# Batch 0 of a fused attention and expert kernel: transposed scores, normalisation by small products, a later read-out, one more DMA transpose, and a first weight chunk loaded in quarters

## The chip, the cores and the metric

The kernel runs on one core of one Trainium2 chip. The metric is the time on the device in microseconds (us); lower is better. Two kernels are compared by runs on the same chip in alternating rounds.

## The reference, cut to what matters

```python
# x (8 batches, 8 heads, 512 rows, 64), state (8, 8, 32, 64)
scores = scale * x @ state^T;  a = softmax(scores);   xread = a @ state        # 512 rows per batch
scores2 = scale * state @ x^T; a2 = softmax(scores2); sread = a2 @ x           # 32 rows per batch
y = concat([xread, sread], rows), heads side by side                           # (8 * 544, 512)
out = gelu(y @ w_in) @ w_out                                                   # w_in 512x2048, w_out 2048x512
```

Two facts shape the kernel. `scores2` is `scores` transposed, so one exponential E serves both reads. And `xread @ w_in` equals `a @ (state @ w_in)`, so the kernel multiplies the small `state` into `w_in` first (the tile P) and never forms `xread`.

## The kernel before

For each batch it computes E = exp(scores), normalises it to A, transposes A to AT, forms P, then `hp = P^T AT` (L470), its GELU `g`, and `op = g^T w_out` (L519, or L564 for parts of batch 0). `sread` ("the read-out") takes E and x to sums of 32 rows. All loads of weights and x go out from GpSimd in one queue, in program order, and are written as bf16:

```python
    load_w_in(0, 512)            # first w_in chunk: two halves (t = 0, 1) of 64 partitions, 512 columns
    load_w_out(0)
    load_w_in(512, 1024)
    load_st(1, 2)
    def load_rest():
        load_x(1)
        load_w_out(1)
        for f in range(2, FC):
            load_w_in(512 * f, 512 * f + 512)
            load_w_out(f)
        ...
```

Batch 0 is prepared in four parts of two heads. Rows of x lie on partitions, so the sum for the normalisation runs along the free dimension, on VectorE; GpSimd multiplies one half, and A is then transposed on TensorE:

```python
    def scores0(q):
        pc = ps_o.tile([128, SJ, 2 * NS], FP32, name="pc", tag="op")
        for j in range(SJ):
            nc.tensor.matmul(pc[:, j, :], lhsT=xT0[:, q, j, :], rhs=sb0[...], start=True, stop=True)
        nc.scalar.activation(out=part0(A.e, q), in_=pc, func=AF.Exp, scale=scale)
    def norm0(t):
        nc.vector.reciprocal(out=ics, in_=A.sums)          # sums from nc.vector.reduce_sum
        eng = nc.gpsimd if t == 0 else nc.vector
        eng.tensor_tensor(out=<A of half t>, in0=<E of half t>, in1=ics.to_broadcast(...), op=ALU.mult)
    def xtr_dma(b):                                        # later batches transpose x and A by DMA
        nc.sync.dma_start_transpose(out=A.xT..., in_=A.x4...)
```

The order of work around the read-out of batch 0 and the burst of P chunks:

```python
    xtr(1, (0, 1)); xtr(1, (2, 3))      # x of batch 1, needs its load
    sread(0); sread_out(0)              # read-out of batch 0
    M(7); scores(1, 0); scores(1, 1)
    srt(0)
    U(4, 5)                             # op, needs the second w_out piece
    rearr_ones(1)
    U(6)
    pmat(0, 2)                          # P from the third w_in piece
    ...
    burst([(1, 3), (2, 0), (2, 1)])     # at 40 us
```

The softmax here doesn't subtract the row's maximum and nothing guards it: scores larger than these inputs give would overflow.

## Time and profile before

| | kernel before |
|---|---|
| time, median of 3 runs | 215.29 us (215.14 to 215.52) |
| profiled span | 213.6 us |
| TensorE busy | 209.2 us, 98% of the span |
| first w_in halves landed | 8.28 and 9.63 us |
| second w_out piece landed | 21.14 us |
| third w_in piece, two halves landed | 22.00 and 23.28 us |

The page of a profile gives busy times and the chain that ended last; the chain of waits lists that chain's pieces in time as start, duration, engine, tile, line and count. A line such as L519 is the kernel's own. The prediction below shows the first 24 us of this chain. For the later reading these pieces are needed as well; they are from the chain of the kernel before:

```profile
23.93 0.34 PE p_ps L408 x8
24.27 0.97 PE op L519 x4
...
39.99 0.77 PE p_ps L408 x24
40.76 0.97 PE op L519 x4
```

The third w_in piece is used at 23.93 and had landed at 23.28, so TensorE had 0.65 us to spare there. The burst at 39.99 runs its 24 products without a gap.

### The profile page before, as it was taken

Reading aid. Unit: us, or ns where it says so; the run is one execution under the profiler, and the core shown is the slowest. Engines: PE = TensorE matmul, PEld = TensorE weight load, DVE = VectorE, ACT = ScalarE, POOL = GpSimd, SP = SyncE. Lnnn points to the kernel's source line nnn. Section 1 sums busy time; section 2 is a strip of 40 time slices with the busy share of each in tenths; the row PEclk is TensorE's granted clock in tenths of the full one; section 3 lists DMA queues with packets and bytes.
Section 4 is the critical chain, followed back from the end, with each engine's and each line's share of the span. In section 5 each row is a group of like instructions: output and inputs, shape, how many; then the busy total and the mean of one; then the engine's idle time right before and its main releaser. Section 6 shows DMA issues by size and latency. Waiting matters only on the chain.

```text
span 213.6 us, 4028 instructions
## 1 busy us (share of the span) xinstructions
PE 209.2 (98%) x1674; PEld 103.7 (49%) x1674; DVE 81.3 (38%) x169; ACT 122.5 (57%) x218; POOL 43.5 (20%) x57
## 2 busy tenths in 40 slices
PE   8999999999999999999999999999999999999994
PEld 7735444444444445444444444444444444765443
DVE  3835675723059102940177006900393026000151
ACT  3765855797777448844974467645864444864000
POOL 7573304901213013302321230300000000000000
PEclk9999999999999999999999999999999999999999
DMA  7999999983722691439350963170222014000034
GB/s 182 172 200 205 206 193 161 220 178 51 96 98 101 122 123 50 150 60 144 47 196 4 155 90 139 60 146 5 98 100 54 0 40 158 3 0 0 10 105 183
DMA packets 39731, 22.98 MB, mean 108 GB/s; under 512 B 22048, under 2 KB 36384, under 8 KB 39712
## 3 DMA queue, kind: packets, MB, share of 16 engines
q0 software_dynamic: 13664, 8.23, 27.8%
q1 hardware_dynamic: 25360, 14.09, 24.6%
q10 hardware_dynamic: 688, 0.39, 0.6%
q8 instruction: 13, 0.21, 0.4%
q14 instruction: 6, 0.05, 0.1%
HBM read 17.30 MB, written 8.91 MB: 123 GB/s over the span
## 4 chain that ended last, share of the span: by engine, by line
PE 97%; POOL 0%; ACT 0%; issue 0%; DVE 0%
PE op L519 47%; PE hp L470 25%; PE p_ps L408 4%; PE op L564 3%; PE hps L534 3%; PE ops L546 3%; PE warm_ps L133 2%; PE opl L497 2%; PE pt L316 2%; PE sr L371 1%; PE hp L624 1%; PE aT_ps L353 1%; PE xT_ps L239 1%; POOL a L303 0%; PE xT_ps L258 0%; PE pc L279 0%
## 5 line engine op out<-in xcount | busy, mean ns | idle before, releaser
L519 PE MATMUL op<-w_out_bf,g 128*128 128x512 bf16 x464 | 110.1, 379 | 0.0
L477 ACT ACTIVATE g<-hp 128x512 bf16<-128x512 f32 x124 | 66.5, 600 | 52.8 <-PE hp L470 52.7
L519 PEld LDWEIGHTS <-g 128*128 128x128 bf16 x464 | 44.9, 98 | 54.3 <-issue 1.5
L470 PE MATMUL hp<-AT,P 128*128 128x512 bf16 x248 | 63.4, 379 | 0.0
L483 DVE COPY osb<-op 128x512 f32<-128x512 f32 x31 | 21.4, 691 | 85.0 <-PE op L519 85.0
L470 PEld LDWEIGHTS <-P 128*128 128x128 bf16 x248 | 22.8, 98 | 25.2 <-ACT P L419 0.5
L419 ACT CAST P<-p_ps 128x512 bf16<-128x512 f32 x31 | 16.3, 595 | 12.5 <-PE p_ps L408 12.5
L420 DVE CAST P<-p_ps 128x512 bf16<-128x512 f32 x31 | 19.9, 682 | 6.0 <-PE p_ps L408 5.9
L202 POOL COPY x<-xb 128x1024 bf16<-128x1024 bf16 x12 | 12.2, 1043 | 31.9 <-DMA xb<-in_x_dram 26.5
L212 POOL COPY xo<-xb 128x1024 bf16<-128x1024 bf16 x12 | 12.2, 1049 | 21.7 <-PE sr L371 21.7
L336 DVE TENSOR_REDUCE cs<-e 128x16 f32<-128x512 bf16 x14 | 9.5, 678 | 4.0 <-ACT e L323 4.0
L323 ACT ACT_TABLE_LOAD x7 | 9.0, 1283 | 1.8 <-issue 1.3
L408 PE MATMUL p_ps<-w_in_bf,sbd 64*32 64x512 bf16 x248 | 9.9, 381 | 0.0
L483 DVE COPY osb<-ops 128x512 f32<-128x512 f32 x2 | 1.4, 692 | 22.5 <-PE ops L546 22.5
L339 DVE TENSOR_TENSOR a<-e,ics 128x512 bf16<-128x512 bf16 x14 | 9.7, 692 | 0.5
L477 ACT ACT_TABLE_LOAD x7 | 9.0, 1283 | 0.1
L508 ACT COPY osb<-opl 128x128 f32<-128x128 f32 x1 | 0.3, 266 | 15.2 <-PE opl L497 15.2
L133 PE MATMUL warm_ps<-warm 128*128 128x128 bf16 x66 | 7.0, 275 | 1.0 <-DVE warm L80 1.0
L564 PE MATMUL op<-w_out_bf,g 128*128 128x512 bf16 x32 | 7.8, 380 | 0.0
L323 ACT ACTIVATE e<-pt 128x512 bf16<-128x512 f32 x14 | 7.6, 594 | 0.1
L534 PE MATMUL hps<-XSR,w_in_bf 128*128 128x256 bf16 x64 | 7.6, 273 | 0.0
L546 PE MATMUL ops<-w_out_bf,g_sr 128*128 128x512 bf16 x32 | 7.1, 379 | 0.0
(80 smaller groups left out, 118.9 us busy)
## 6 DMA issues: line engine op xcount, KB each, us to landing
out_dram<-osb SPq DMA_DIRECT2D x24, 256.0 KB, 2.3
xb<-in_x_dram POOLq DMA_DIRECT2D x7, 512.0 KB, 6.2
w_in_bf<-in_moe_w_in_dram POOLq DMA_DIRECT2D x8, 256.0 KB, 10.1
w_out_bf<-in_moe_w_out_dram POOLq DMA_DIRECT2D x4, 512.0 KB, 11.6
out_dram<-osb SPq DMA_DIRECT2D x14, 128.0 KB, 2.0
x0f<-in_x_dram SPq DMA_DIRECT2D x2, 256.0 KB, 3.5
out_dram<-osb SPq DMA_DIRECT2D x8, 64.0 KB, 1.7
x0f<-in_x_dram ACTq DMA_DIRECT2D x1, 256.0 KB, 4.2
```

The lines of the kernel that those rows point to most:

```text
L202: nc.gpsimd.tensor_copy(out=A.x4[:, :, :, 64 * t:64 * t + 64].rearrange("p j c d -> p c j d"), in_=src[:, t],)
L323: nc.scalar.activation(out=A.e[:, :, 64 * half:64 * half + 64], in_=pt.rearrange("p j t c n -> p (j t) (c n)"), func=AF.Exp, scale=scale,)
L408: nc.tensor.matmul(ps[t][32 * c:32 * c + 32, :], lhsT=sbd[64 * t:64 * t + 64, b, c, 32 * t:32 * t + 32], rhs=w_in_bf[64 * t:64 * t + 64, c ...
L419: nc.scalar.copy(out=dst[:, 0, :], in_=ps[0])
L420: nc.vector.tensor_copy(out=dst[:, 1, :], in_=ps[1])
L470: nc.tensor.matmul(hp, lhsT=Ps[b][:, t, m * 128:(m + 1) * 128], rhs=atts[b].AT[:, :, t, :], start=(t == 0), stop=(t == 1),)
L477: nc.scalar.activation(out=gs[b][:, m, :], in_=hp, func=AF.Gelu)
L483: nc.vector.tensor_copy(out=osb, in_=ps)
L519: nc.tensor.matmul(ps, lhsT=gs[b][:, m, j * 128:(j + 1) * 128], rhs=w_out_bf[:, m, :], start=(m == 0), stop=(m == MC - 1),)
L534: nc.tensor.matmul(hp, lhsT=w_in_bf[:, c, m * 128:(m + 1) * 128], rhs=XSR[:, c, :], start=(c == 0), stop=(c == HC - 1),)
L546: nc.tensor.matmul(ps, lhsT=g_sr[:, m, s * 128:(s + 1) * 128], rhs=w_out_bf[:, m, :], start=(m == 0), stop=(m == MC - 1),)
L564: nc.tensor.matmul(ops[b, j], lhsT=gs[b][:, m, j * 128:(j + 1) * 128], rhs=w_out_bf[:, m, :], start=(m == 0), stop=(m == MC - 1),)
```

## The change

Its intent is to shorten the preparation of batch 0 and to keep GpSimd out of it. The scores are computed transposed (state rows on partitions, x rows along the free dimension), so that E comes out as ET and AT needs no transposes. The sums over state rows are then products with a block of ones; the reciprocals, split into two bf16 parts, are spread over partitions by 32 small products per half. The read-out needs E the other way round; a DMA transpose supplies it, and the read-out moves to the burst at 40 us. The first w_in chunk is loaded in quarters.

```diff
-    load_w_in(0, 512)
+    load_w_in(0, 256, (0,))
+    load_w_in(256, 512, (0,))
+    load_w_in(0, 256, (1,))
+    load_w_in(256, 512, (1,))
 ...
     def scores0(q):
+        t = q // 2                     # pcs[t]: one [128, 512] tile per half
+        nc.tensor.matmul(pcs[t][h, :], lhsT=sb0[:, t, q % 2, ...], rhs=xT0[:, q, ...], ...)
+        if q % 2 == 1:
+            nc.scalar.activation(out=eT0[:, t, :], in_=pcs[t], func=AF.Exp, scale=scale)
+    def sums0(t):                      # 4 products with bones, then reciprocal and its remainder
     def norm0(t):
-        eng = nc.gpsimd if t == 0 else nc.vector
+        ps = ps_o.tile([128, S], FP32, name="rb", tag="op")
+        for j in range(SJ):
+            for i, r in enumerate((r0_hi(t), r0lo[:, t, :, :])):
+                for c in range(HC):
+                    nc.tensor.matmul(ps[32 * c:32 * c + 32, 128 * j:128 * j + 128],
+                        lhsT=r[:, j, c:c + 1].to_broadcast((128, NS)), rhs=ident, ...)
+        nc.vector.tensor_tensor(out=A.AT[:, :, t, :], in0=eT0[:, t, :]..., in1=ps..., op=ALU.mult)
+    def e0_dma():
+        nc.sync.dma_start_transpose(out=e0, in_=eT0.rearrange("p t s -> p (t s)"))
 ...
-    sread(0)
-    sread_out(0)
     M(7)
 ...
-    srt(0)
     U(4, 5)
 ...
     mm2_m(0, 11)
+    e0_dma()
     begin(2)
 ...
-    burst([(1, 3), (2, 0), (2, 1)])
+    burst([(1, 3), (2, 0), (2, 1)], 0)
```

Cut: tiles, the casts and evictions that change between ScalarE and VectorE, the counts of the filler products (`keep_warm`), the later place of `srt(0)`, and that `load_rest()`, which issues the later loads, stands earlier in the program.

More of the change, by code (lines that the diff above doesn't have):

```diff
@@ L64 @@
     sb0 = persist.tile([128, 2, 2, 2, NS], BF16, name="sb0")
+    e0 = persist.tile([128, 2 * SJ, 128], BF16, name="e0")
+    eT0 = persist.tile([128, 2, S], BF16, name="eT0")
+    xo0 = persist.tile([128, SJ, HC, 132], BF16, name="xo0")
+    bones = persist.tile([128, HC], BF16, name="bones")
+    r0 = persist.tile([128, 2, SJ, HC], FP32, name="r0")
+    r0lo = persist.tile([128, 2, SJ, HC], BF16, name="r0lo")
     gate = persist.tile([128, HC], FP32, name="gate")
@@ L85, with load_w_in @@
     nc.vector.memset(sb0, 0.0)
-    for i in range(2):
-        nc.vector.memset(xos[i][:, :, :, 1:2], 1.0)
-        nc.vector.memset(xos[i][:, :, :, 130:131], 1.0)
-    def load_w_in(f0, f1):
-        for t in range(2):
+    nc.vector.memset(bones, 0.0)
+    for c in range(HC):
+        nc.vector.memset(bones[32 * c:32 * c + 32, c:c + 1], 1.0)
+    for xo in xos + [xo0]:
+        nc.vector.memset(xo[:, :, :, 1:2], 1.0)
+        nc.vector.memset(xo[:, :, :, 130:131], 1.0)
+    def load_w_in(f0, f1, ts=(0, 1)):
+        for t in ts:
             nc.gpsimd.dma_start(
@@ L127, in load_rest @@
         load_x(3)
+    warm_ps = ps_o.tile([128, 512], FP32, name="warm_ps", tag="op")
     def keep_warm(n):
-        ps = ps_o.tile([128, 512], FP32, name="warm_ps", tag="op")
         for _ in range(n):
-            nc.tensor.matmul(ps[:, 0:128], lhsT=warm, rhs=warm, start=True, stop=True)
+            nc.tensor.matmul(warm_ps[:, 0:128], lhsT=warm, rhs=warm, start=True, stop=True)
     def state_prep(b0, b1):
@@ L171, in state0 @@
             h = slice(64 * u, 64 * u + 64)
-            nc.vector.tensor_copy(out=sb0[h, :, :, u, :], in_=ps[h, 0:2, u:HC:2, :])
+            nc.scalar.copy(out=sb0[h, :, :, u, :], in_=ps[h, 0:2, u:HC:2, :])
         return ps
@@ L189, in begin @@
         A.x4 = x4s[b % 2]
-        A.xo = xos[b % 2]
-        if b > 0:
-            A.xT = att.tile([128, SJ, HC, 128], BF16, name="xT", tag="xT")
+        A.xo = xos[b % 2] if b else xo0
+        if b == 0:
+            A.e = e0
+            A.AT = att.tile([128, SJ, 2, 128], BF16, name="AT", tag="AT")
+            return
+        A.xT = att.tile([128, SJ, HC, 128], BF16, name="xT", tag="xT")
         A.e = att.tile([128, SJ * 2, HC * NS], BF16, name="e", tag="e")
@@ L218, in cast0 @@
     def cast0(q):
-        copy = nc.scalar.copy if q == 1 else nc.vector.tensor_copy
-        copy(
+        nc.vector.tensor_copy(
             out=x0b[:, q, :, :, :].rearrange("p j u d -> p u j d"),
@@ L246, in xtr0 @@
                 )
-        copy = nc.scalar.copy if q == 2 else nc.vector.tensor_copy
-        copy(out=xT0[:, q, :, :], in_=ps)
+        nc.vector.tensor_copy(out=xT0[:, q, :, :], in_=ps)
     def xtr(b, cs):
@@ L268, in xtr_dma @@
         )
-    def part0(x, q):
-        v = x.rearrange("p (j t) f -> p j t f", t=2)[:, :, q // 2, :]
-        return v[:, :, 64 * (q % 2):64 * (q % 2) + 64]
+    pcs = {}
     def scores0(q):
-        A = atts[0]
-        pc = ps_o.tile([128, SJ, 2 * NS], FP32, name="pc", tag="op")
+        t = q // 2
+        if q % 2 == 0:
+            pcs[t] = ps_o.tile([128, S], FP32, name="pc", tag="op")
+        h = slice(64 * (q % 2), 64 * (q % 2) + 64)
+        nc.tensor.matmul(
+            pcs[t][h, :],
+            lhsT=sb0[:, t, q % 2, :, :].rearrange("p u n -> p (u n)"),
+            rhs=xT0[:, q, :, :].rearrange("p j n -> p (j n)"),
+            start=True,
+            stop=True,
+        )
+        if q % 2 == 1:
+            nc.scalar.activation(out=eT0[:, t, :], in_=pcs[t], func=AF.Exp, scale=scale)
+    def sums0(t):
+        ps = ps_f.tile([128, SJ, HC], FP32, name="cs0", tag="f")
         for j in range(SJ):
             nc.tensor.matmul(
-                pc[:, j, :],
-                lhsT=xT0[:, q, j, :],
-                rhs=sb0[:, q // 2, q % 2, :, :].rearrange("p u n -> p (u n)"),
+                ps[:, j, :],
+                lhsT=eT0[:, t, 128 * j:128 * j + 128],
+                rhs=bones,
                 start=True,
@@ L285, in scores0, with r0_hi @@
             )
-        nc.scalar.activation(out=part0(A.e, q), in_=pc, func=AF.Exp, scale=scale)
-    def sums0(q):
-        A = atts[0]
-        if q % 2 == 0:
-            A.sums = att.tile([128, SJ, HC], FP32, name="cs", tag="cs")
-        nc.vector.reduce_sum(
-            out=A.sums[:, :, q % 2 * 2:q % 2 * 2 + 2],
-            in_=part0(A.e, q).rearrange("p j (c n) -> p j c n", n=NS),
-            axis=AX.X,
-        )
+        nc.vector.reciprocal(out=r0[:, t, :, :], in_=ps)
+        nc.vector.tensor_tensor(
+            out=r0lo[:, t, :, :], in0=r0[:, t, :, :], in1=r0_hi(t), op=ALU.subtract
+        )
+    def r0_hi(t):
+        v = r0.rearrange("p t j c -> p (t j c)").bitcast(BF16)
+        return v.rearrange("p (t j c w) -> p t j c w", t=2, j=SJ, w=2)[:, t, :, :, 1]
     def norm0(t):
         A = atts[0]
-        ics = att.tile([128, SJ, HC], FP32, name="ics", tag="ics")
-        nc.vector.reciprocal(out=ics, in_=A.sums)
-        eng = nc.gpsimd if t == 0 else nc.vector
-        eng.tensor_tensor(
-            out=A.a.rearrange("p (j t) (c n) -> p j t c n", t=2, n=NS)[:, :, t, :, :],
-            in0=A.e.rearrange("p (j t) (c n) -> p j t c n", t=2, n=NS)[:, :, t, :, :],
-            in1=ics[:, :, :].to_broadcast((128, SJ, HC, NS)),
+        ps = ps_o.tile([128, S], FP32, name="rb", tag="op")
+        for j in range(SJ):
+            for i, r in enumerate((r0_hi(t), r0lo[:, t, :, :])):
+                for c in range(HC):
+                    nc.tensor.matmul(
+                        ps[32 * c:32 * c + 32, 128 * j:128 * j + 128],
+                        lhsT=r[:, j, c:c + 1].to_broadcast((128, NS)),
+                        rhs=ident,
+                        start=(i == 0),
+                        stop=(i == 1),
+                    )
+        nc.vector.tensor_tensor(
+            out=A.AT[:, :, t, :],
+            in0=eT0[:, t, :].rearrange("p (j n) -> p j n", j=SJ),
+            in1=ps.rearrange("p (j n) -> p j n", j=SJ),
             op=ALU.mult,
         )
+    def e0_dma():
+        nc.sync.dma_start_transpose(out=e0, in_=eT0.rearrange("p t s -> p (t s)"))
     def scores(b, half):
@@ L372, in sread @@
                         A.sr[32 * c:32 * c + 32, t, :],
-                        lhsT=A.e[:, 2 * j + t, 32 * c:32 * c + 32],
+                        lhsT=A.e[:, 2 * j + t if b else SJ * t + j, 32 * c:32 * c + 32],
                         rhs=A.xo[:, j, c, 1 + 65 * t:66 + 65 * t],
@@ L429, in burst @@
         done = []
-        first = len(chunks) < 4 and b_read is not None
+        first = len(chunks) < 3 and b_read is not None
         if first:
@@ L583 @@
     cast0(0)
+    xtr0(0)
     st0 = state0()
-    xtr0(0)
     cast0(1)
     state0_p(st0)
-    keep_warm(7)
+    keep_warm(6)
     cast0(2)
@@ L592 @@
     xtr0(2)
-    keep_warm(4)
+    xtr0(3)
     scores0(1)
-    sums0(0)
-    xtr0(3)
     keep_warm(2)
     scores0(2)
-    keep_warm(4)
+    keep_warm(2)
+    scores0(3)
+    load_rest()
+    keep_warm(3)
+    sums0(0)
+    pmat00(0)
+    keep_warm(2)
     sums0(1)
     norm0(0)
-    scores0(3)
-    sums0(2)
-    sums0(3)
+    pmat00(1)
     norm0(1)
-    load_rest()
-    keep_warm(8)
-    pmat00(0)
     nc.scalar.activation(out=gate, in_=gate, func=AF.Gelu)
-    keep_warm(5)
-    atr(0, (0,))
-    keep_warm(4)
-    pmat00(1)
-    atr(0, (1,))
     for q in range(4):
@@ L721 @@
                 load_x(b + 3)
-            if p == 3 and b > 1:
-                srt(b)
+            if p == 3:
+                srt(b if b > 1 else 0)
     while u < 16 * B - 4:
```

## The prediction

> **What bounds the kernel now.** I read the page first, then the chain of waits of the first 25 us, then the timeline there, then the DMA view.
>
> ```profile
> PE 209.2 (98%) x1674; PEld 103.7 (49%) x1674; DVE 81.3 (38%) x169; ACT 122.5 (57%) x218; POOL 43.5 (20%) x57
> ...
> PE 97%; POOL 0%; ACT 0%; issue 0%; DVE 0%
> ```
>
> TensorE is busy 98% of the span and carries 97% of the chain that ends last. So only two things can help: fewer matmuls, or an earlier start of the unbroken stream. The change touches the head, where batch 0 is prepared. The chain of waits there (start us, us, what):
>
> ```profile
> 8.77 0.39 ACT e L286
> 9.16 1.05 POOL a L303
> ...
> 11.53 1.75 PE hp L624 x8
> ...
> 13.33 2.76 PE op L564 x12
> 16.09 0.34 PE p_ps L408 x8
> ...
> 18.75 1.01 PE xT_ps L258 x32
> 19.77 0.36 PE sr L371 x31
> 20.12 0.54 PE hp L470 x2
> 20.66 0.47 PE pt L316 x16
> 21.13 0.21 PE srT L395
> 21.34 2.59 PE op L519 x12
> ```
>
> The chain leaves TensorE once: exp (0.39), then GpSimd's normalising product (1.05). The change aims at this spot. From 11.53 on nothing waits; sr and srT, batch 0's read-out, lie on the chain.
>
> A second bound lies just beneath. The timeline gives the issue of two loads and the last exchange of activation tables; the DMA view gives the us from each load's issue to its landing:
>
> ```profile
> 10.14 0.96 POOL L104 DMA_DIRECT2D xb<-in_x_dram  x1
> 10.16 1.28 ACT L609 ACT_TABLE_LOAD   x1
> ...
> 11.10 0.76 POOL L100 DMA_DIRECT2D w_out_bf<-in_moe_w_out_dram  x1
> ...
> 12.67 2.06 ACT L632 ACTIVATE g<-hp 128x512 bf16<-128x512 f32 x4 [0.54 <-PE hp L624]
> ```
> ```profile
> xb<-in_x_dram POOLq DMA_DIRECT2D x1, 512.0 KB, 8.1
> ...
> w_out_bf<-in_moe_w_out_dram POOLq DMA_DIRECT2D x1, 512.0 KB, 10.0
> ```
>
> Sums of start and landing time: xb for batch 1 lands at 18.2 and is used at 18.75; the second w_out piece lands at 11.10 + 10.0 = 21.1 and is used at 21.34 (L519). By the same sums the first w_in halves land at 8.3 and 9.65 (used at 9.1 and 10.9), the first w_out piece at 12.25 (used at 13.33), the second w_in piece at 15.3 (used at 16.09). The slack is 0.2 to 1.1 us everywhere, and smallest at L519. And the stream has no gaps; the DMA view from 9 to 22 us:
>
> ```profile
> DMA packets 3420, 2.63 MB, mean 203 GB/s; under 512 B 383, under 2 KB 3419, under 8 KB 3419
> ...
> q0 software_dynamic: 3419, 2.62, 129.8%
> ```
>
> 203 GB/s are written as bf16, so 406 GB/s are read as fp32. Each next load lands when its bytes have passed, whenever it was issued.
>
> **What the Trainium skill says.** "DMA: Bandwidth & Descriptors", section Issuing engines are not separate DMA queues: DMAs from the scalar, sync and gpsimd engines run on the same 16 engines and interleave. No load of the trace before meets a transpose on another queue, so it neither shows nor denies this; the whole DMA argument rests on it. "ScalarE: Activation LUTs", section What ACT_TABLE_LOAD costs: about 1283 ns plus about 1380 ns of drain. The trace agrees on the load (mean 1283) but not on the drain: the gate activation began at 11.45, right after the load of 10.16. "TensorE: Matmul & The Clock Gate", Part 3 (packing): matmuls of 32 output columns in different column groups run together. The trace agrees: 32 sr matmuls of 65 columns take 0.36 us in the chain, 11 ns each.
>
> **The change part by part.**
>
> *Head, up to the first GELU.* Removed: GpSimd's product (1.05), four row sums on VectorE (0.42, 0.41, 0.69 for two), two groups of A transposes (0.40 each) with their evictions (0.42 each). Added: two exp of 128x512 instead of four of 128x256 (about 0.6 each, as L323); two groups of 4 tiny sum products (estimate 0.4 with latency); two reciprocals (0.25) and two subtractions (estimate 0.15); two groups of 32 products, 32 columns wide, with a moving operand of 128 (estimate from sr: 32 x 128/65 x 11 ns = 0.7 at most, 0.5 likely); two products on VectorE out of PSUM (0.69, as L339). Walking the new order from the x pieces' landings (3.82, 5.1, 5.4, 5.9) with these durations and about 0.1 us per hand-over: casts on VectorE end at 4.3, 5.9, 6.35; transposes evicted at 5.5, 7.1, 7.8, 8.2; exps end at 8.3 and 9.3; first reciprocal 9.35, remainder 9.55; first spread 9.7 to 10.3, product to 11.1; second P product right behind the first spread at 10.2, its copy on ScalarE ends near 11.15; second spread to 11.1, product to 11.85. Transposed-scores products on TensorE (L656) can then run at 11.2 and 12.05.
>
> But the table load now stands behind **both** P copies: 11.15 + 1.28 + 0.2 for the gate = 12.65. Before, it ran between the copies and the first GELU was at 12.67. So the second stage of the chain (L564 at 13.33) starts where it did, plus or minus 0.3. The hole is shorter, and ScalarE takes its place.
>
> *First w_in chunk in quarters.* Same bytes, same order; four issues of 0.63 us instead of two. The second P product still needs both last quarters. I give it nothing: bytes set the landing. The following loads' issue moves ahead of 10.14 because GpSimd no longer multiplies, but the queue was never empty, so that gives nothing either.
>
> *E by DMA transpose.* It stands late in the program, but the order on SP puts it directly behind the x loads, and its one wait is for ScalarE's second exp. So it will go out near 9.3, not at 34 us. A transpose of the same 256 KB, in the timeline before, and what its queue did from 51 to 52.4 us (packets, MB, share of 16 engines):
>
> ```profile
> 49.93 1.23 SPq L359 DMA_TRANSPOSE AT<-a  x1
> ```
> ```profile
> q1 hardware_dynamic: 1030, 0.26, 98.3%
> ```
>
> First packets come about 1.1 us after issue and occupy 98% of 16 engines for 1.4 us. They will run from about 10.4, in the middle of the gapless load stream, and push everything behind it by 0.3 (bytes alone, part in overlap) to 1.3 us (all of it); I take **0.9**. Then xb lands at 19.1 and the second w_out piece at 22.0.
>
> *Read-out later.* sr (0.36) and srT (0.21) leave the stretch before L519. TensorE would reach L519 at 21.34 - 0.57 = 20.77, but must wait for w_out. Both come back after 40 us, on the chain: sr 0.36, srT 0.06 (as in other batches). The burst that takes sr has three chunks, and sr needs a PSUM buffer that ScalarE's first copy frees:
>
> ```profile
> 39.92 0.84 PE L408 MATMUL p_ps<-w_in_bf,sbd 64*32 64x512 bf16 x24
> ```
>
> In the chain its products end at 40.76; the first copy there starts at 40.39 and takes 0.59, to 40.98, plus hand-over: a wait of some 0.25.
>
> *Sum.* Start of L519: 21.14 + 0.9 + 0.05 - 21.34 = +0.75. Read-out re-added: 0.36 + 0.06 + 0.25 = +0.67. Total +1.4: 215.3 + 1.4 = 216.7. I lean a little lower, to **216.4**, because a retuned order suggests gains that I may not see.
>
> **The rivals.** *The head really gets shorter and the loads follow.* For it: GpSimd's detour goes. For it to count, the first GELU and the w_out landing must both move earlier; the load rate sags from 5 to 8 us (about 130 GB/s against 203), and quarters might mend that by up to 0.8. Then L519 starts at 20.8 to 21.1 and the time is 214.9 to 215.6. Against: the table load, and the same bytes. *The transpose costs the loads nothing.* If the engines have room beside a stream that memory limits, the landings stay, and the time is 215.3 - 0.15 + 0.67 = 215.8. For it: packets of q0 overlap (129.8%). *The transpose takes its full share, and the loads behind it stack up*: +1.3 - 0.15 + 0.67 gives 217.1; with smaller packets in the quarters, up to 217.4.
>
> **Range and chances.** The three give 214.9 to 217.4. 2% is 4.3 us; the whole affected head is only 13 us long and its start can't move by that much either way. Faster 0.01, same 0.98, slower 0.01.
>
> **What would show it.** Right: the transpose of E issued near 9.3; loads behind it landing later than before by 0.3 to 1.3; TensorE idle just before xT of batch 1 and above all before the second w_out piece is used; the first GELU still near 12.6, directly behind table load and gate; sr in the 40 us burst waiting for a copy by ScalarE. Wrong: the second w_out piece landing before 21, or the first GELU before 12.2. The prediction fails if the slow start of w_in goes away in quarters, or if the transpose moves through unnoticed.

## The result, and the profile after

| | before | after |
|---|---|---|
| time, median of 4 runs in the same rounds | 215.41 us (215.14 to 216.13) | 218.92 us (218.47 to 219.40) |
| ratio, after over before | | 1.0158, 95% interval 1.0120 to 1.0196 |
| profiled span | 213.6 us | 216.7 us |

The ratio is the mean time of one kernel's runs over that of the other's of the same rounds, so it is not quite the ratio of the medians. Executions in which one die ran at a lower clock are left out of the means. The change costs 1.6%, which is inside the 2% called "same", but the time lies 1.5 us above the predicted range.

First the page of the kernel after, in its lines of busy times and of the chain's shares:

```profile
PE 209.5 (97%) x1707; PEld 102.7 (47%) x1707; DVE 80.4 (37%) x173; ACT 121.7 (56%) x216; POOL 43.7 (20%) x58
PE 86%; DMA 7%; POOL 4%; ACT 0%; issue 0%; POOLq 0%
```

TensorE's busy time hardly moved (209.2 to 209.5 us), but a DMA now holds 7% of the chain that ends last. Before, none did. The waits of TensorE in the kernel after name the loads (waiting engine and line, what it waited for, us in total, times, longest):

```profile
PE xT_ps L272 <- DMA xb<-in_x_dram: 1.2, 1, 1.2
...
PE p_ps L446 <- DMA w_in_bf<-in_moe_w_in_dram: 0.6, 1, 0.6
PE sr L409 <- ACT P L457: 0.3, 1, 0.3
```

The timeline of the kernel after gives the head (issue of the transpose, table load, first GELU, start of the stream):

```profile
9.07 1.39 SPq L346 DMA_TRANSPOSE e<-eT  x1
...
10.93 1.28 ACT L646 ACT_TABLE_LOAD   x1
...
12.34 2.04 ACT L664 ACTIVATE g<-hp 128x512 bf16<-128x512 f32 x4
12.97 2.76 PE L602 MATMUL op<-w_out_bf,g 128*128 128x512 bf16 x12 [0.25 <-ACT g L664]
```

The first GELU is at 12.34 (before 12.67) and the unbroken stream of TensorE starts at 12.97 (before 13.33). These 0.36 us are not a shown gain: over all traces the stream starts at 12.97 to 13.60 with the new head (after, e1, e6 to e9) and at 12.71 to 13.62 with the old one (before, e2 to e5, e10, e11). In this run they were lost within 7 us to the wait for xb. The transpose of E was issued at 9.07, although it stands far later in the program: nothing on SP's own queue stood before it, and its only wait, for the second exponential, had ended. It landed at 18.63.

The chain of the kernel after, from the last load on it to the burst:

```profile
10.11 15.63 DMA w_in_bf<-in_moe_w_in_dram
25.74 0.04 issue
25.78 0.41 PE p_ps L446 x7
...
41.90 0.41 PE p_ps L446 x8
42.31 0.58 ACT P L457
42.90 0.04 issue
42.94 0.43 PE sr L409 x30
43.37 0.97 PE op L557 x4
```

The third w_in piece landed at 25.74 and its products began at 25.78, against 23.93 before: **+1.85**. In the burst, the time from the first p_ps to the next op was 43.37 - 41.90 = 1.47, against 40.76 - 39.99 = 0.77 before: **+0.70**. A single transpose (srT) after the burst adds **0.06**. The last piece of the two chains, before and after:

```profile
210.68 0.27 ACT osb L508
```
```profile
213.35 0.27 ACT osb L546
```

It moved by 2.67, of which these three terms make 2.61. From the last store's landing to the end of the span there were 0.93 us before and 1.36 after: **+0.43**. The sum is 3.1, which is the growth of the span. Two of the four timed runs were slower than the profiled one by another 0.9 us; they have no trace.

Finally the load stream. The DMA view gives packets, MB and share of 16 engines by queue; q0 holds the loads and q1 the transpose. The kernel after from 11 to 13 us (loads alone), and from 13.4 to 18.1 us:

```profile
DMA packets 300, 0.29 MB, mean 145 GB/s; under 512 B 17, under 2 KB 300, under 8 KB 300
```
```profile
q0 software_dynamic: 1180, 0.56, 91.1%
q1 hardware_dynamic: 1050, 0.26, 46.5%
```

In the kernel before the loads moved 0.40 MB from 11 to 13, and 0.93 MB from 13.4 to 18.1. At the mean rate of 203 GB/s the loads thus lost ground twice: (0.40 - 0.29) / 0.203 = 0.5 us before the transpose's packets appeared (the first at 13.4, the last at 18.1), and (0.93 - 0.56) / 0.203 = 1.8 us while they ran. By bytes moved, the loads were 0.6 us ahead of the kernel before at 10 us, level at 12.5, and 1.9 us behind from 19 us to 30 us.

### The profile page after: what moved, and what is told of

It reads as the page before. It is cut to its first block, busy times and chain, and to the rows that moved or that the text cites. A ratio compares the mean times of both kernels' runs of the same rounds, so it can differ in the third digit from the quotient of the medians.

```text
span 216.7 us, 4095 instructions
## 1 busy us (share of the span) xinstructions
PE 209.5 (97%) x1707; PEld 102.7 (47%) x1707; DVE 80.4 (37%) x173; ACT 121.7 (56%) x216; POOL 43.7 (20%) x58
## 4 chain that ended last, share of the span: by engine, by line
PE 86%; DMA 7%; POOL 4%; ACT 0%; issue 0%; POOLq 0%
PE op L557 45%; PE hp L508 24%; DMA w_in_bf<-in_moe_w_in_dram 7%; PE p_ps L446 4%; PE hps L572 3%; PE ops L584 3%; POOL w_in_bf L101 2%; PE op L602 2%; PE opl L535 2%; PE sr L409 1%; PE pt L354 1%; POOL w_out_bf L109 1%; POOL xb L113 0%; POOL x0c L85 0%; POOL st_bf L117 0%
## 5 line engine op out<-in xcount | busy, mean ns | idle before, releaser
L228 POOL COPY xo<-xb 128x1024 bf16<-128x1024 bf16 x12 | 12.2, 1050 | 22.5 <-PE sr L409 22.5
L361 ACT ACT_TABLE_LOAD x7 | 9.0, 1283 | 1.4 <-issue 1.3
L515 ACT ACT_TABLE_LOAD x7 | 9.0, 1283 | 0.1
L572 PEld LDWEIGHTS <-w_in_bf 128*128 128x128 bf16 x64 | 6.3, 98 | 1.6
```

The source lines that it names most:

```text
L228: eng.tensor_copy(out=A.xo[:, :, :, 2 + 64 * t:66 + 64 * t].rearrange("p j c d -> p c j d"), in_=src[:, t],)
L361: nc.scalar.activation(out=A.e[:, :, 64 * half:64 * half + 64], in_=pt.rearrange("p j t c n -> p (j t) (c n)"), func=AF.Exp, scale=scale,)
L515: nc.scalar.activation(out=gs[b][:, m, :], in_=hp, func=AF.Gelu)
L572: nc.tensor.matmul(hp, lhsT=w_in_bf[:, c, m * 128:(m + 1) * 128], rhs=XSR[:, c, :], start=(c == 0), stop=(c == HC - 1),)
```

## The experiments

The theory: **the transpose of E**, issued in the middle of a saturated load stream, delays the loads by more than its own bytes, and TensorE waits for them. The rivals: the later read-out is the loss; the quarters are; one more DMA changes the end of the program; an instruction fetch holds up one load. Runs e1 to e4 shared their runs of the kernel before (median 215.31 without the slow run), so did e5 to e8 (215.59) and e9 to e11 (215.30). The ratio's interval decides; n is 4 runs each (6 in e9). All gave the right result.

| run | time, median (range) | ratio to before (95%) | span |
|---|---|---|---|
| after | 218.92 (218.47 to 219.40) | 1.0158 (1.0120 to 1.0196) | 216.7 |
| e1, transpose held back | 216.54 (216.45 to 217.03) | 1.0054 (1.0027 to 1.0081) | 214.8 |
| e2, before + idle transpose | 217.97 (217.62 to 218.94) | 1.0123 (1.0085 to 1.0162) | 216.5 |
| e3, before + quarters | 215.06 (214.93 to 215.31) | 0.9982 (0.9957 to 1.0008) | 213.5 |
| e4, before + late read-out | 216.29 (215.70 to 216.99) | 1.0049 (1.0012 to 1.0085) | 213.9 |
| e5, before + tiny DMA | 216.06 (215.26 to 216.75) | 1.0020 (0.9982 to 1.0058) | 214.3 |
| e6, after, fetch moved | 219.08 (218.28 to 219.76) | 1.0149 (1.0107 to 1.0190) | 218.0 |
| e7, after, E by TensorE | 215.55 (215.37 to 215.64) | 0.9997 (0.9968 to 1.0025) | 213.7 |
| e8, after, no quarters | 219.72 (219.30 to 220.24) | 1.0192 (1.0157 to 1.0228) | 217.6 |
| e9, e7 + more quarters | 215.64 (215.12 to 216.23) | 1.0006 (0.9983 to 1.0030) | 213.9 |
| e10, before + half the idle transpose | 216.92 (216.75 to 217.17) | 1.0067 (1.0041 to 1.0092) | 215.1 |
| e11, before + plain copy | 216.96 (216.42 to 217.39) | 1.0059 (1.0027 to 1.0092) | 215.6 |

### e1_hold: the transpose held back

The kernel after, with one element of the transpose's target written by GpSimd first, from data that exists only at about 28 us. It makes the transpose wait; the result is unchanged.

```diff
     mm2_m(0, 11)
+    nc.gpsimd.tensor_copy(out=e0[:, 0, 0:1], in_=gs[0][:, 11, 0:1])
     e0_dma()
```

> The changed kernel with one more wait: the DMA transpose of E may start only when chunk 11 of batch 0's GELU is there (near 28 us), behind the loads that the stream waits for. Theory (the transpose takes bandwidth from the loads): the second half of the third w_in piece lands near 23.3 to 24 us instead of 25.74, TensorE's wait for it goes away, and the time falls by 1.8 to 2.6 us against the changed kernel, to about 0.5 to 1.2 us above the kernel before. Rival (the lost time is the moved read-out, the new head and the quarters, not the transpose): the time stays within 0.5 us of the changed kernel.

The transpose went out at 28.61. The loads landed like before or earlier (xb 17.95, second w_out piece 20.49, third w_in piece 21.81 and 23.07), and from 11 to 13 us they moved 0.41 MB, about as before (0.40). No DMA is left among TensorE's waits. The time fell from 218.92 to 216.54, by ratios from +1.58% to +0.54%, which is 2.2 us. What is left is the read-out and the tail: the chain is 0.79 us late after the burst (hp at 45.58, before 44.79), and from the last landing to the end of the span it takes 1.34 us instead of 0.93. So the **collision is 2.2 to 2.4 us of the 3.5**. Note that e1 does not remove the collision. It moves it: the two loads of x that were then under way landed at 36.59 and 39.71 (before 34.86 and 37.85), but TensorE did not wait for them.

The chain of waits of e1 also shows what replaced the removed read-out:

```profile
19.02 0.59 PE xT_ps L272 x16
...
19.62 1.30 DVE xT L273 x2
...
21.38 2.59 PE op L557 x12
```

VectorE's eviction of xT, which the removed read-out used to cover, is now on the chain, and op begins at 21.38 where it began at 21.34 before. The stream of this run started at 13.59, later than before, so e1 does not tell what an earlier start would be worth.

### e2_extra_transpose: the transpose alone

The kernel before, with one more DMA transpose of 256 KB from E into a tile that nobody reads.

```diff
+    ed = persist.tile([128, 2 * SJ, 128], BF16, name="ed")
     mm2_m(0, 11)
+    nc.sync.dma_start_transpose(out=ed, in_=atts[0].e.rearrange("p g f -> p (g f)"))
```

> The kernel before, with nothing changed but one DMA transpose of 256 KB of batch 0's E into a tile that nobody reads, free to start at the fourth exp (near 9.2 us). Theory (collision): its packets alternate with the loads', the loads behind it land 1.5 to 2 us later, and the time rises by 1.3 to 2.5 us. Rival (a transpose moves beside the loads unnoticed): the time stays within 0.4 us of the kernel before.

Issue at 8.85, packets from 13.2 to 18.6, landing at 19.0. The waits of TensorE in e2, and from its timeline the two later ones for weights:

```profile
PE xT_ps L259 <- DMA xb<-in_x_dram: 1.0, 1, 1.0
...
PE p_ps L409 <- DMA w_in_bf<-in_moe_w_in_dram: 0.6, 1, 0.6
PE op L520 <- DMA w_out_bf<-in_moe_w_out_dram: 0.3, 1, 0.3
```
```profile
16.96 0.41 PE L409 MATMUL p_ps<-w_in_bf,sbd 64*32 64x512 bf16 x7 [0.57 <-DMA w_in_bf<-in_moe_w_in_dram]
...
23.63 2.75 PE L520 MATMUL op<-w_out_bf,g 128*128 128x512 bf16 x12 [0.26 <-DMA w_out_bf<-in_moe_w_out_dram]
```

TensorE waits for loads as in the kernel after, without any of its other parts, but not for all the same ones: here for the second w_in piece, for xb, and last for the second w_out piece (used at 23.63, before at 21.34); for the third w_in piece it doesn't wait. The loss is 217.97 - 215.31 = 2.7 us, slightly more than the 2.5 expected at most, and 0.43 of it is the tail. The transpose alone reproduces the main loss.

### e3_quarters and e8_whole_chunk: the quarters

e3 is the kernel before with the quarters; e8 is the kernel after with the two halves.

```diff
-    load_w_in(0, 512)
+    load_w_in(0, 256, (0,))
+    load_w_in(256, 512, (0,))
+    load_w_in(0, 256, (1,))
+    load_w_in(256, 512, (1,))
```

> The kernel before, with only the first w_in chunk loaded in quarters. Theory: the slow start of w_in from 5 to 7.5 us goes away (first chunk complete near 9.0 instead of 9.63, first w_out piece near 11.6 instead of 12.24), but a like sag comes at the next w_in piece, so that the second w_out piece lands at 21.1 plus or minus 0.3 and the time stays within 0.5 us. Rival (quarters speed the whole stream up): everything lands 0.6 us earlier, and the time falls by at most 0.2, since TensorE has no wait there. Second rival (smaller packets cost): landings and time later by 0.5 us or more.

> The changed kernel with the first w_in chunk loaded in two halves as before. Theory: the slow start of w_in is back at 5 to 7.5 us, the later sag at 11 to 12.5 goes, and the stream ends up where it was, so the time stays within 0.6 us of the changed kernel (the instruction fetch may fall on another load and shift this). Rival (the quarters cost by their smaller packets or by more waits on GpSimd): the time falls by 1 us or more.

e3: no difference. The loads were 0.5 us ahead at 7.5 us and level at 11.5. e8: xb landed at 20.68 (after: 19.52), the third w_in piece at 24.50 and 26.59, and TensorE waited for both. It is slower than the kernel after by ratios of 1.0192 against 1.0158, some 0.7 us (0.6 at most was expected), with intervals that overlap. So no part of the loss is seen to come from the quarters. Whether they help in the new kernel is open: e8's loads were 2.6 us behind the kernel before at 20 us, against 1.9 in the kernel after, but e6 below has the quarters and was 3.0 behind. The head start of about 0.6 us at 10 us fades by itself: without any transpose it was gone by 16 us in e7 and down to 0.2 in e1.

### e4_late_read: the read-out alone

The kernel before with batch 0's read-out in the burst at 40 us and its own tile for it.

```diff
-    sread(0)
-    sread_out(0)
     M(7)
-    srt(0)
     U(4, 5)
-    burst([(1, 3), (2, 0), (2, 1)])
+    burst([(1, 3), (2, 0), (2, 1)], 0)
```

> The kernel before, with only batch 0's read-out moved to the burst near 40 us (its own xo tile, E stays in its pool buffer). Theory: the second w_out piece still lands near 21.1, so TensorE gains at most 0.2 us ahead of it, and pays 0.36 for sr, 0.25 to 0.35 for the wait for ScalarE's first copy in the burst and 0.06 for srT: the time rises by 0.4 to 0.8 us. Rival (the read-out is the same work wherever it stands): within 0.2 us.

The waits of TensorE in e4 have these two:

```profile
PE sr L372 <- ACT P L420: 0.3, 1, 0.3
...
PE op L520 <- DMA w_out_bf<-in_moe_w_out_dram: 0.2, 1, 0.2
```

The first is the wait for ScalarE's copy that was predicted. The second shows that with the read-out gone from the early stretch, TensorE reaches the second w_out piece before it lands. The span grew by 0.3 (213.9), the time by 0.98 in the medians, with an interval of 0.3 to 1.8 us by the ratio. The late read-out is a small loss without any collision; its size between 0.3 and 1.0 is not settled by these runs.

### e5_small_dma: one more DMA

The kernel before with a DMA of 16 rows of 256 bytes on SP near 4 us.

```diff
+    tiny = persist.tile([128, 64], FP32, name="tiny")
     mm2_m(0, 11)
+    nc.sync.dma_start(out=tiny[0:16, :], in_=st_f[0:16, 0, :])
```

> The kernel before with one more, tiny DMA on SP (16 rows of 256 bytes, near 4 us, read by nobody). The eight completion semaphores of SP's and ScalarE's DMAs are dealt out in turn, and the waits at the end of the program test them in the order 0 to 7; the kernel before ends with its last store on semaphore 7, with one more DMA it is on 0, so that seven further waits follow after the last landing. Theory: the stretch from the last store's landing to the end of the span grows from 0.93 to about 1.35 us, and the time by 0.4 us, with nothing changed earlier. Rival: the 0.4 us in the changed kernel's end has another cause, and this kernel is within 0.15 us of the one before.

In the compiled program eight completion semaphores are dealt in turn to the DMAs of SP and ScalarE, and the end of the program tests them in order. With 64 such DMAs the last store has the last semaphore; with 65 it has the first, and seven more tests follow. From the last landing to the end of the span e5 took 1.34 us. Every traced kernel with the 65th DMA took 1.34 to 1.36 us (after, e1, e2, e5, e6, e8, e10, e11); every one without took 0.91 to 0.93 (before, e3, e4, e7, e9). At the end of the kernel after, SP's eight tests start 0.06 us apart, from 215.35 to 215.79. The 0.43 us are thus shown in the traces. The time (ratio 1.0020) neither shows nor excludes them.

### e6_fetch_later: the instruction fetch

The trace has records of 16 KB on a queue of instructions, one about every 250 TensorE instructions. In the kernel after one falls into the load of the third w_in piece (DMA view of 23.2 to 24.3 us):

```profile
q8 instruction: 1, 0.02, 5.4%
```

It occupied one of the 16 engines for 0.95 us, and that piece's second half landed 2.44 us after the first, not 1.28 as before. e6 is the kernel after with fewer, larger filler products at the start (48 TensorE instructions less, each product being an instruction and a weight load), so that the fetch comes later.

```diff
-    keep_warm(32)
+    keep_warm(8, 512)     # 8 products of 512 columns
```

> The changed kernel with its first 32 warm-up products of 128 columns replaced by 8 of 512 columns: 48 fewer TensorE instructions ahead of everything, about the same time on the array. Theory: the 16 KB instruction fetch that occupied one DMA engine from 23.3 to 24.2 us belongs to TensorE's instruction stream, so it moves to 26 us or later; the second half of the third w_in piece then lands near 24.6 instead of 25.74, TensorE's wait in front of its P products shrinks, and the time falls by 0.7 to 1.2 us against the changed kernel. Rival (that half is late because the transpose left one engine behind): it still lands near 25.7, and the time stays within 0.3 us.

The fetch moved from 23.28 to 26.45, and the halves landed at 24.44 and 25.72, 1.28 apart again. The time did not fall. The stream as a whole was later in this run (3.0 us behind at 20 us), and the waits of TensorE show the loss in another place:

```profile
PE xT_ps L272 <- DMA xb<-in_x_dram: 1.9, 1, 1.9
```

The fetch explains why this load and no other was the last wait in the kernel after. It doesn't explain the loss of the kernel as a whole: the expected 0.7 to 1.2 us did not come back.

### e7_pe_transpose and e9_more_quarters: a version without the DMA transpose

e7 is the kernel after with E taken back by eight TensorE transposes in the hole before the first GELU, and the read-out in its old place. e9 adds quarters for the second w_in chunk.

```diff
-        nc.sync.dma_start_transpose(out=e0, in_=eT0.rearrange("p t s -> p (t s)"))
+        for t in range(2):
+            for j in range(SJ):
+                nc.tensor.transpose(ps[:, SJ * t + j, :], eT0[:, t, 128 * j:128 * j + 128], ident)
+        nc.vector.tensor_copy(out=e0, in_=ps)
```

> The changed kernel with E transposed by eight TensorE transposes right behind the second spread (0.45 us in a hole of the head) and evicted by VectorE, and with the read-out back at its old place; no DMA transpose, quarters kept. Theory: no collision, no read-out wait in the burst, last store on semaphore 7 again; the first GELU stays at 12.3 to 12.7, the second w_out piece lands near 20.5 to 20.8, its use starts at 20.9 to 21.4, and the time is 214.7 to 215.5, within 0.3 us of the kernel before or slightly faster. Rival (the new head itself costs): 216 or more.

> The kernel of e7_pe_transpose with the second w_in chunk in quarters too, in search of a version that beats the kernel before. Theory: in e7 the sag of the loads moved from 5 to 7.5 us to the next whole w_in piece (11 to 13 us); with that piece in quarters too it may go for good, the second w_out piece lands near 20.3 and the third w_in piece near 22.8 to 23.2; TensorE follows by at most 0.3 us: 214.9 to 215.4, about 0.1 to 0.3 us faster than the kernel before, which may not be told from noise. Rival (the sag only moves on to the next load, or the smaller packets cost): the same as e7 within 0.2 us or slower.

e7 equals the kernel before (0.9997), and so does e9 (1.0006, five rounds). The new way to prepare batch 0 costs nothing and gives nothing. In e7 the stream started at 13.13 instead of 13.33 (in e9 at 13.60), the second w_out piece landed at 20.72 and the halves of the third w_in piece at 22.04 and 24.00 (a fetch fell between them), so the products that need it began at 23.73 but took 0.72 us in the chain instead of 0.34. In e9 the second w_out piece landed at 21.03, not near 20.3 as hoped. No version is shown to beat the kernel before.

### e10_half_transpose and e11_plain_copy: what in the transpose costs

e10 halves e2's transpose; e11 copies the same 256 KB without transposing, in rows of 2 KB.

```diff
 e10
+    nc.sync.dma_start_transpose(out=ed[:, 0:SJ, :], in_=atts[0].e.rearrange("p g f -> p (g f)")[:, 0:512])
 e11
+    nc.sync.dma_start(out=ed, in_=atts[0].e)
```

> The kernel before with one extra DMA transpose of half the size (128 KB, 512 packets of 256 bytes) at the same place as in e2. Theory (the cost goes by packets, each of which takes a turn on an engine): the loads fall behind by about half of what e2 showed (e2: 1.9 to 2.4 us, here 0.9 to 1.2), and the time rises by 0.8 to 1.6 us, of which 0.4 is the last store's semaphore. Rival (a fixed cost of having a transpose among the loads): as e2, 2.3 us or more.

> The kernel before with the same 256 KB of E moved at the same place by a plain DMA copy in rows of 2 KB instead of a transpose. Theory (packets, not bytes, set the cost): some 128 packets; the loads fall behind by 0.3 to 0.9 us and the time rises by 0.4 (semaphore) to 1.2 us. Rival (bytes set the cost): as e2, the loads 1.9 us behind and the time 2.3 us up or more.

Bytes of the loads (q0) in the two windows tell the loss, at 203 GB/s against the kernel before (losses from unrounded bytes):

| run | 11 to 13 us, MB | 13 to 19 us, MB | loss before packets, us | loss while they run, us |
|---|---|---|---|---|
| before | 0.40 | 1.20 | | |
| e3, e7, e1 (no DMA on SP there) | 0.38, 0.39, 0.41 | 1.16, 1.11, 1.14 | 0.0 to 0.1 | 0.2 to 0.4 |
| after | 0.29 | 0.81 | 0.5 | 1.9 |
| e2, transpose of 256 KB | 0.26 | 0.74 | 0.7 | 2.2 |
| e10, transpose of 128 KB | 0.32 | 0.96 | 0.4 | 1.2 |
| e11, copy of 256 KB | 0.28 | 1.04 | 0.6 | 0.8 |

The DMA views of 13 to 19 us of e2 and of e11 show what differs (queue, packets, MB, share of 16 engines):

```profile
q0 software_dynamic: 1386, 0.74, 95.4%
q1 hardware_dynamic: 1056, 0.26, 45.0%
```
```profile
q0 software_dynamic: 1810, 1.04, 121.6%
q1 hardware_dynamic: 144, 0.26, 13.4%
```

The same 0.26 MB are 1024 packets of 256 bytes as a transpose (32 of q1's are others) and 128 of 2 KB as a copy, and the copy takes a third of the loss while it runs. Half the transpose takes half. So that loss goes with the size of a transpose and is not a fixed cost, and it is not set by the bytes alone. Whether the number of packets makes it or the transposing itself, these runs do not separate. The earlier loss, from 11 to 13 us, is 0.3 to 0.7 us in all runs with a large DMA on SP (e6 0.3, e8 0.4), whether it transposes or not, and at most 0.1 in those without (e4 and e9 0.1). The later loss scatters by 0.4 among the runs without, so smaller differences there say little. What the engines do in that time has no records in the trace: that stays open. In all, the loads were 1.3 us behind the kernel before at 20 us in e10 and in e11 alike, and in time the two can't be told apart (1.0067 and 1.0059). e11's expectation, at most 0.9 behind and 1.2 us slower, was thus missed, and that packets alone set the whole cost is not shown.

## Why the prediction was wrong

**The mechanism was right, its size was not.** The transpose did go out near 9.3 (9.07), did meet the load stream, and TensorE did wait for loads: held back (e1) it gave 2.2 us back, added alone (e2) it cost 2.2 us without the tail. The time is 2.5 us above the predicted 216.4, and these steps of the prediction failed or held:

- **The failing step: "I take 0.9" for the delay of the loads, of at most 1.3, carried no further than the second w_out piece.** The packets were to run from about 10.4, for the 1.4 us that another transpose took alone. They ran from 13.4 to 18.1, 4.7 us, beside about as many packets of the loads. A packet took 33 ns (46.5% x 16 x 4.7 us / 1050), against 21 alone (98.3% x 16 x 1.4 us / 1030). At 20 us 2.51 MB of the loads had gone out, against 2.95 in e1, the same kernel with the transpose held back: 0.44 / 0.203 = 2.2 us of delay. The prediction had the duration alone as its upper limit; that was no limit when two queues shared the engines.
- **The place of the last wait.** The start of the op after xb was predicted at 22.09 and came at 22.08; the second w_out piece was predicted to land at 22.0 and did at 22.04. That this fits is luck. TensorE had waited for xb (landed at 19.52, predicted 19.1) and not for w_out, and with the same transpose the w_out piece landed at 23.59 in e2 and 23.20 in e6. The prediction stopped there and gave no slack for the third w_in piece. Its slack had been 0.65, and its second half landed 2.46 us later than before: 1.30 with its first half, and 1.16 that the fetch on one engine accounts for. This adds 1.85 - 0.75 = 1.1 to the predicted sum.
- **"I give it nothing" for the quarters** was right for the time of the kernel before (e3). What they do inside the new one is not settled (e8, e6).
- **The read-out**, predicted at +0.67 with a wait of 0.25 for ScalarE's copy: +0.76 in the chain (0.70 and 0.06), the wait 0.3. Right.
- **The end of the program** was not looked at: +0.43 (e5 and the tails of all runs).
- **"I lean a little lower"** took off 0.3 for gains that I might not see. There were none.
- **The first GELU** at 12.65: came at 12.34, directly behind the table load and the gate as described. It came at 12.48 to 12.96 in the five other traces with the new head. Right: the head gained nothing that shows.
- **Sums and readings of the prediction that don't hold**, without effect on its 216.4: for the rival of the shorter head, an L519 at 20.8 to 21.1 gives, with its own +0.67 for the read-out, 215.4 to 215.7 and not 214.9 to 215.6. From 5 to 8 us the loads moved 147 GB/s, not about 130. And one load of the kernel before does meet the end of a transpose: from 99 to 100 us 72 packets of the loads pass beside 21 of SP's queue.

With what the profile showed in place of these terms: 216.4 + 0.3 (lean) + 1.1 (third w_in piece) + 0.1 (read-out) + 0.4 (tail) = 218.3, against 218.47 in the profiled run. The remaining 0.5 up to the median of 218.92 lies in two runs without a trace. Traced runs with a transpose of 256 KB at this place had load delays of 1.9 to 3.0 us at 20 us, so such a spread is plausible, but not shown for those two.

The **pages of the Trainium skill** on which the prediction rested the collision and the spread products held: the section "Issuing engines are not separate DMA queues" of "DMA: Bandwidth & Descriptors" says that DMAs of all issuers interleave on 16 engines, and after 13.4 us about 119 packets of the loads and 121 of the transpose pass per 0.5 us around 16 us. "Queues, rings and completion order" of the same page says that an engine takes turns between queues by packets of several descriptors. The even count agrees with taking turns. That taking turns with many small packets is what costs the stream so much would fit e10 and e11, but is argued, not shown. "TensorE: Matmul & The Clock Gate", Part 3, on packing, carried the estimate of the 32 spread products; at 0.5 to 0.7 us it was right, they started at 9.32 and the next product at 9.88.

Left open: why the transpose's packets begin only 4.4 us after its issue (1.2 us in the undisturbed case at 50 us), what slows the loads in the 2 us before, and why the collision cost varies between runs.

## What to carry to other kernels

Before a DMA is added to an early, saturated load stream, list the slack of every load behind it, and don't take a transpose's duration alone as the upper limit of the delay; here 256 KB, 1.4 us alone, cost 2.2 us of load time. The same transpose cost nothing visible where the loads beside it had slack (e1). In this kernel a late place in the program did not hold the transpose back on an idle queue: a wait did (e1). Don't call a start shorter from one trace: here it varied by 0.6 to 0.9 us between runs of like heads. An added DMA can move the last store's place among the final waits.

## What the Trainium skill lacked or had wrong

- "DMA: Bandwidth & Descriptors", "Latency and other measured facts", gives an effective rate of 261 GB/s for a DMA transpose with a non-contiguous middle dimension, and more for a contiguous one. Alone, 0.26 MB took 1.4 us here, some 190 GB/s. There is nothing on its cost beside other traffic: it took 1.9 to 2.2 us from the loads while it ran, a plain copy of the same bytes 0.8, half the transpose 1.2.
- The same page has no figure for the stretch between the issue of a DMA on a busy set of engines and its first packet: 4.4 us here, and from 11 to 13 us in it the loads moved 0.29 MB instead of 0.40.
- "Runtime: NRT & Kernel Launch", "Instruction fetch mechanics", has the refills of 16 KiB, but no page has what one costs a load beside it: one engine for 0.95 us (up to 1.5 in e6), and the load that it met landed 1.16 us later.
- "ScalarE: Activation LUTs", "What ACT_TABLE_LOAD costs": the load of about 1283 ns agrees (1.28 us); the drain of about 1380 ns does not show. The load began at 10.93, 0.01 us after the copy before it, and the gate activation at 12.23, 0.02 us after the load.
- No page has the order of the final waits: the same last store cost 0.93 or 1.36 us from its landing to the end, by its place among eight semaphores.
